# Zero products in TensorE's planned idle stretches, U transfers as single operations, and another score bank for the last tile

## The chip, the cores and the metric

The kernel runs on one core of one Trainium2 chip. The metric is the device time of one execution in microseconds (us). Before the change three runs took 506.69, 511.74 and 516.97 us; their median is 511.74 us. Profiles are of one execution each. Engines are named as in the profile: PE (TensorE's products), PEld (its weight loads), DVE (VectorE), ACT (ScalarE), POOL (GpSimd) and SP (SyncE, which here only issues transfers). A "q" behind an engine's name is its instruction sequencer.

## The reference, cut to what matters

```python
# A: attention with 16 query heads and one key and value head, S = 2048, D = 448, head size 28
q = (x @ wq).reshape(B, S, H, Dh).transpose(0, 2, 1, 3)
k = x @ wk
v = x @ wv
scores = jnp.einsum("bhqd,bkd->bhqk", q, k) * (Dh ** -0.5)
p = softmax(scores, axis=-1)
o = jnp.einsum("bhqk,bkd->bhqd", p, v)
a = o.transpose(0, 2, 1, 3).reshape(B, S, H * Dh) @ wo

# B: a state-space layer as a long convolution, L = 2048, D = 448 channels, N = 256 states
logdA = exp(log_dt)[:, None] * (A_re + 1j * A_im)
P = jnp.exp(logdA[:, :, None] * l[None, None, :])
K = jnp.einsum("dn,dnl,dn->dl", Cc, P, dB).real
y = causal_convolution(u, K) + u * Dskip          # by a Fourier transform in the reference

g = sigmoid((x * gate_w).sum(-1))
out = g * a + (1 - g) * b
```

## The kernel before, in words

**Attention.** The scores are cut into 1024 tiles of 128 keys by 512 query columns, grouped into 410 sets of three and two tiles in turn. `qk` (in `main`) makes a set: PE multiplies keys and queries into score banks of `psS` (L1264 for a set of three, as row-tiled products that run side by side; L1287 for single full products; L1275 and L1278 are the same two for the last 64 tiles, whose columns are cut in halves), and ACT takes the exponential of the whole set into the ring `expT` (L1313). There are five score banks, a tile's bank is its number modulo 5, so one set's products can be made while the other's exponential runs. `pv` (L1331, for the last 64 tiles L1325) multiplies four exponential tiles with the values and sums up in the one bank `psB` (bank 6) over the 16 key blocks of a head group. `norm` then copies that bank out (L1110), and further steps on DVE, POOL's transfers and PE divide by the row sums and project the output (`outp`, L1092). The last query block goes by `scaled` (L1154, L1161) and `last` (L1188, L1192, with the identity product that brings in what the output already holds), and its copy out of `psB` is L1341.

**State-space layer.** For each of 14 groups of 32 channels, `tables` builds tables of powers on DVE (L935, L950, L964 and others), `kgen` multiplies them on PE into the convolution's kernel (L994), and POOL stores this to a scratch tensor in memory, `KP_scratch`. `tload` brings it back as shifted copies: one table load is four transfer issues `T<-KP_scratch` on SP of 272 KB each, 56 loads in all (the late ones go into parts of `U` that are free by then, `U<-KP_scratch`). `conv` (L1054) is the convolution: products of `U`, the shifted inputs, with the loaded table, then DVE (L1063) and PE (L1074) turn the result for the output. `U` holds half of the channels. `ufill` refills a chunk of it for the second half from a copy in `T`: seven transfer issues `U<-T` on SP, a first one of 128 KB and six of 32 KB, in rows of 64 bytes. There are seven such chunks.

**Order.** Nothing is ordered by hand. Every step is recorded as an `Op` with an engine, a planned duration, a priority and its dependences, and `Prog.schedule` runs a list scheduler over all of them: it plays the program through with planned durations and puts each engine's instructions in the order in which they would start (`key = (r, o.pr, i)`). Each engine then executes its list strictly in that order, waiting on semaphores. A transfer counts as `ISSUE` (470 ns on SP) for each issue plus its landing time, and two transfers of one `slot` never overlap. The planner also keeps a model of PE's instruction fetch in blocks (`block`) and, for PE, of switches between tilings (`mode`, `SWITCH`).

PE has a filler already: behind the first 64 sets, `warm` (L1247) multiplies a matrix of 512 columns by columns of `cst` into `psB` with `start=False`, 43 times. Before the first work, L614 multiplies zeros of `cst` by themselves 18 times, L753 spreads one row over the partitions, and L624 turns the input.

Of the kernel before, what the change touches and what calls it, by code (L numbers as in the profile page):

```python
# [12 lines left out]
P = 128  # L13
# [63 lines left out]

class Op:
    __slots__ = ("i", "eng", "fn", "ns", "lat", "deps", "pr", "lock", "unlock", "slot", "ndma",
                 "count", "vc", "end", "comm", "extra", "mode", "ni")  # L80


class Prog:
# [9 lines left out]
    POOL = (7, 5)  # L93
    SLACK = {"pe": 500.0, "dve": 300.0}
    FAR = 2500.0

    def __init__(self, nc, es):
        self.nc, self.es = nc, es
        self.ops = []
        self.lastw = {}  # L100
        self.readers = {}
        self.slots = {}
        self.commops = {}
        self.after = {}

    def op(self, eng, fn, ns, rd=(), wr=(), pr=0, lat=None, lock=None, unlock=None, comm=None, mode="f", ni=0):
        o = Op()
        o.i, o.eng, o.fn, o.ns, o.lat, o.pr = len(self.ops), eng, fn, ns, 0, pr
        o.lock, o.unlock, o.slot, o.ndma = lock, unlock, None, 0
        o.comm = comm  # L110
        o.mode, o.ni = mode, ni
        o.lat = self.LAT[eng] if lat is None else lat
        deps = {}
        if comm is not None:
            for k in comm:
                deps[self.lastw[k]] = 1
                self.commops.setdefault(k, []).append(o.i)
        for k in rd:
            for c in self.commops.get(k, ()):
                deps[c] = 1  # L120
            w = self.lastw.get(k)
            if w is not None:
                deps[w] = 1
        for k in wr:
            w = self.lastw.get(k)
            if w is not None:
                deps[w] = 1
            for r in self.readers.get(k, ()):
                deps.setdefault(r, 0)
        for k in rd:  # L130
            self.readers.setdefault(k, []).append(o.i)
        for k in wr:
            self.lastw[k] = o.i
            self.readers[k] = []
        deps.pop(o.i, None)
        o.deps = deps
        self.ops.append(o)
        return o

    def dma(self, pairs, desc, slot, rd=(), wr=(), pr=0, eng="sp", slow=False, extra=0, fac=1.0):  # L140
        kw = dict(allow_slow_non_contiguous=True) if slow else {}

        def fn(e):
            return [e.dma_start(o, i, **kw) for o, i in pairs]  # L144
        nd, size = desc
        ns = 15.0 if size <= 64 else 13.0 + 0.033 * size if size < 1500 else 8.0 + 0.0372 * size
        o = self.op(eng, fn, nd * ns * fac / 16.0 * (1.15 if size < 1500 else 1.8 if nd < 512 else 1.0), rd, wr, pr)
        o.slot, o.ndma, o.extra = slot, len(pairs), extra
        prev = self.slots.get(slot)
        if prev is not None:  # L150
            o.deps[prev] = 1
        self.slots[slot] = o.i
        return o
# [11 lines left out]
    def schedule(self):  # L165
# [23 lines left out]
        done = 0  # L189
        npe = 0  # L190
        block = [0.0, 0.0]
        for o in ops:
            if o.eng == "pe":
                o.ni = self.count(o)
        while done < n:
# [24 lines left out]
            assert best is not None, "scheduler stuck"  # L220
            (r, _, _), e, i = best
            o = ops[i]
            ready[e].remove(i)
            if e == "pe" and o.mode != mode:
                r = max(r, free[e] + self.SWITCH)
                mode = o.mode
            if e == "pe":
                npe += o.ni
                while npe > self.FIRST + (len(block) - 2) * self.BLOCK:
                    block.append(r + (self.FETCH if dmafree > r else self.IDLE))  # L230
# [15 lines left out]
                o.lock.bank = L[3]  # L246
                L[2] = []
            if o.slot is not None:
                free[e] = r + self.ISSUE[e] * o.ndma
                s = r if e == "pool" else max(r, dmafree)  # L250
                end = max(s + o.ns, free[e]) + self.DMA_NS + o.extra
                dmafree = max(dmafree, s) + o.ns
            else:
                ns = o.ns
                if e == "pe" and self.HALF[0] < r < self.HALF[1]:
                    ns *= self.HALF[2]
                free[e] = r + ns
# [129 lines left out]
class Kernel:  # L387
# [182 lines left out]
    def prep_u(self):  # L570
# [15 lines left out]
        for k, (c0, c1) in enumerate(((0, 2), (2, 5), (5, 9), (9, 14))):  # L586
            n = 16 * (c1 - c0)
            pg.dma(self.ushift(self.U, 1024 * c0, self.U, 1024 * c0, 128, n, 1), (6 * 16 * n, 64), f"du{k}", rd=[("Ub", 0), ("Ub", 1)],
                   wr=[("Uc", c) for c in range(c0, c1)], pr=0.35 if k < 2 else 0.9 + 0.1 * k, slow=True)
        V0 = lambda b, off, n, r: b.v(0, P, off, [[n // r, r], [1, n // r]])  # L590
        Z = lambda n, r: self.cst.v(0, P, 512, [[0, r], [1, n // r]])
        pg.dma([(V0(self.O, 0, 16 * D, 32), Z(16 * D, 32))], (4096, 448), "zO", rd=[("cst", 1)] + done,
# [426 lines left out]
    def tload(self, gi):  # L1019
# [8 lines left out]
        for h in range(4):  # L1028
            to = bass.AP(tensor=buf.h, offset=h * rs + o, ap=[[4 * rs, 32], [TC, 8], [1, TC]])
            lst.append((to, dram(self.KP, h * 512 + 1 + 8 * gi * KW, [[1, 32], [KW, 8], [1, TC]])))  # L1030
        pg.dma(lst, (1024, 1088), f"T{s}", rd=[("KP", gi // 4, gi % 4 // 2), "pad", "kp0"] + x, wr=w, pr=1, extra=1500)

    def ufill(self, c):
        pg = self.pg
        lst = [(self.U.v(0, P, c * 2048, [[128, 16], [1, 32]]), self.T.v(0, P, UB + c * 512, [[32, 16], [1, 32]]))]
        lst += self.ushift(self.U, c * 2048, self.T, UB + c * 512, 32, 32, 1)
        pg.dma(lst, (5120, 64), f"uf{c % 4}", rd=[("UB", 0), ("UB", 1), ("yx", 2 * c + 5)], wr=[("Uc", 2 * c), ("Uc", 2 * c + 1)], pr=1.2, slow=True)

    def conv(self, c):
        pg = self.pg  # L1040
# [3 lines left out]
        for k in range(4):  # L1044
# [5 lines left out]
            for n in range(8):  # L1050
                def mm(e, k=k, n=n, to=to, gi=gi, tbuf=tbuf):
                    m0, par = 2 * (n // 2), n % 2
                    for j in range(4):
# [3 lines left out]
                                     start=(n == 0), stop=(n == 7), tile_position=(0, 32 * j), skip_group_check=True)  # L1057
                    return r
                first = k == 0 and n == 0
                pg.op("pe", mm, 56, mode="c", ni=8, rd=[("T", s), ("Uc", c % 14), ("Ub", 0), ("Ub", 1)],  # L1060
                      wr=[X] + ([("cst", cs)] if first else []), pr=1.6,
                      lock=ps if first else None)
        pg.op("dve", lambda e: e.tensor_tensor(self.cst.v(0, P, cs * 512, [[128, 4], [64, 2], [1, 64]]),  # L1063
# [107 lines left out]
    def last(self):  # L1171
        pg = self.pg
        for half in range(2):
            m1, m2 = self.scaled(half)
            for tt in range(2 * half, 2 * half + 2):
# [17 lines left out]
                                                                 tile_position=(0, 0), skip_group_check=True), 200,  # L1193
                          rd=[("O", tl), ("Oz", tl), "id"], wr=[Y] + key, pr=1, lock=F)
                if half:
                    pg.after[o.i] = end
                for g in range(3):
                    o = pg.op("pe", lambda e, mm=mm, g=g: mm(e, g), 200, rd=["Wo", ("on", g)],
                              wr=[Y] + key, pr=1)
# [26 lines left out]
    def main(self):  # L1226
# [13 lines left out]
        for ts in sets:  # L1240
            bs, es = sorted(t % 5 for t in ts), sorted(t % RING for t in ts)
            for t, b, x in zip(ts, bs, es):
                bank[t], ring[t] = b, x
        spread = lambda x, n: [[512 * (x[1] - x[0]), n], [1, 512]] if n > 1 else [[1, 512]]

        def warm(e):
            return e.matmul(self.psB.v(0, P, 0, [[1, 512]]), self.cst.v(0, P, 512, [[1, P]]),  # L1247
                            self.ident.v(0, P, 0, [[0, 4], [1, P]]), start=False, stop=False,
                            tile_position=(0, 0), skip_group_check=True)

        def qk(s):
            ts = sets[s]
# [64 lines left out]
        def pv(v):  # L1317
            ts = range(4 * v, 4 * v + 4)

            def mm(e):  # L1320
# [14 lines left out]
            pg.op("pe", mm, 230, rd=["va"] + [("e", ring[t]) for t in ts], wr=[("b", 6)], pr=0.5, mode="c", ni=8)  # L1335
            i, kt, h = dec(4 * v)
            if kt == 15 and i < 15:
                self.norm(i)
            if i == 15 and v % 8 == 7:
# [81 lines left out]
```

## Time and profile before

| | us |
|---|---|
| median of three runs | 511.74 |
| the profiled execution: time | 512.68 |
| its span, first to last instruction | 510.7 |
| PE busy / idle in the span | 443.5 / 67.2 |
| ACT busy | 485.6 |
| DVE busy | 457.6 |
| POOL busy | 167.5 |
| mean granted clock of PE, of full speed | 0.967 |

How to read it: busy time is the union of an engine's instructions. Ends of PE's products are modelled, so PE's busy time contains some of its pipeline. Rows of groups read "line engine operation, output<-input, shape xcount | busy us, mean ns of one | idle time of the engine just before them, and what ended it". Rows of the timeline begin with start and duration in us; a bracket at their end holds the engine's idle time before the row and what ended it. Neighbouring instructions of one line are merged in it ("x31"). `PEclk` is the clock that PE was granted, in tenths of full speed, over 40 equal slices of the span.

### The profile page before, as it was taken

The numbers are of one execution on the slowest core, as the hardware profiler recorded it, in microseconds if no ns is written. First come the engines' busy times: TensorE is split into PE (matmuls) and PEld (weight loads), VectorE is DVE, ScalarE is ACT, GpSimd is POOL, SyncE is SP. The second block draws the span as 40 slices with busy tenths as digits, with TensorE's granted clock in tenths as the row PEclk, the third lists the DMA queues.
The fourth block names the chain that finished last, engine by engine and source line by source line (L and its number), as shares of the span: only waits on it lengthen the run. The fifth ranks groups of instructions, "written<-read, shape, count | busy, mean of one in ns | idle before, by whom it ended". The sixth has DMA issues, their size and how long they took to land.

```text
span 510.7 us, 17103 instructions
## 1 busy us (share of the span) xinstructions
PE 443.5 (87%) x7468; PEld 202.9 (40%) x7558; DVE 457.6 (90%) x862; ACT 485.6 (95%) x435; POOL 167.5 (33%) x308
## 2 busy tenths in 40 slices
PE   8897788898888999889788979988888799899986
PEld 6522232243432445433343423443344243445552
DVE  5999999999999999999999969999999989992122
ACT  5999999999998999999999969999999899999984
POOL 5208334224133324215214223521514330624110
PEclk9799999999997999999999979999999799999999
DMA  8996399838427587974848666495672953777931
GB/s 259 323 167 176 40 201 147 246 91 256 135 60 250 144 235 143 300 149 111 176 142 251 135 215 151 110 321 119 187 167 86 300 132 133 217 230 211 338 98 45
DMA packets 151526, 91.84 MB, mean 180 GB/s; under 512 B 83514, under 2 KB 147436, under 8 KB 151452
## 3 DMA queue, kind: packets, MB, share of 16 engines
q1 hardware_dynamic: 141962, 81.05, 59.7%
q0 software_dynamic: 8960, 9.54, 7.8%
q8 instruction: 59, 0.97, 0.8%
q10 hardware_dynamic: 530, 0.17, 0.1%
q14 instruction: 15, 0.12, 0.1%
HBM read 73.61 MB, written 5.23 MB: 154 GB/s over the span
## 4 chain that ended last, share of the span: by engine, by line
ACT 57%; PE 22%; DVE 14%; DMA 4%; issue 2%; SPq 1%
ACT expT L1313 56%; DMA T<-KP_scratch 4%; PE psS L1287 4%; PE psS L1264 3%; DVE tab L935 3%; PE psB L1331 3%; PE psS L1054 2%; DVE tab L950 2%; PE psX L1054 1%; SPq L144 1%; PE psX L994 1%; PE psX L1092 1%; DVE tab L964 1%; PE psX L842 1%; DVE msq L881 1%
## 5 line engine op out<-in xcount | busy, mean ns | idle before, releaser
L1313 ACT ACTIVATE expT<-psS 128x1024 bf16<-128x1024 f32 (+1 forms) x410 | 466.7, 1336 | 13.4 <-PE psS L1264 6.8
L935 DVE TENSOR_TENSOR tab<-tab,mbf 128x512 bf16<-128x512 bf16 (+4 forms) x140 | 140.4, 1006 | 0.1
L1287 PE MATMUL psS<-qM,kT 128*128 128x512 bf16 x305 | 101.3, 393 | 24.9 <-ACT expT L1313 13.1
L1331 PE MATMUL psB<-expT,vaug 128*32 128x512 bf16 x960 | 97.4, 399 | 1.6 <-DVE acc L1110 1.3
L1264 PE MATMUL psS<-qT,kT 29*128 29x512 bf16 x570 | 76.7, 394 | 24.6 <-ACT expT L1313 22.8
L144 POOL DMA_DIRECT2D KP_scratch<-kstg x112 | 61.9, 559 | 104.9 <-DVE kstg L1004 104.6
L950 DVE TENSOR_TENSOR tab<-tab 128x256 bf16<-128x256 bf16 (+4 forms) x140 | 77.7, 578 | 0.0
L144 POOL DMA_DIRECT2D qM<-qT x64 | 32.3, 513 | 73.5 <-DVE qT L854 50.4
L1331 PEld LDWEIGHTS psB<-expT,vaug 128*32 128x32 bf16 x960 | 24.3, 93 | 78.4 <-issue 74.3
L144 POOL DMA_DIRECT2D rdenB<-R_scratch x60 | 31.2, 527 | 59.9 <-DMA R_scratch<-denT 59.8
L1264 PEld LDWEIGHTS psS<-qT,kT 29*128 29x128 bf16 x570 | 18.7, 91 | 67.6 <-ACT expT L1313 57.8
L1054 PE MATMUL psS<-T,U 128*26 128x128 bf16 (+3 forms) x1664 | 41.1, 229 | 4.2 <-DMA T<-KP_scratch 2.4
L1287 PEld LDWEIGHTS psS<-qM,kT 128*128 128x128 bf16 x390 | 24.1, 98 | 44.8 <-ACT expT L1313 29.9
L1054 PEld LDWEIGHTS psS<-T,U 128*26 128x26 bf16 (+3 forms) x1664 | 31.2, 109 | 20.3 <-issue 12.5
L1054 PE MATMUL psX<-T,U 128*26 128x128 bf16 (+3 forms) x1600 | 37.7, 225 | 1.1 <-DMA T<-KP_scratch 0.8
L1054 PEld LDWEIGHTS psX<-T,U 128*26 128x26 bf16 (+3 forms) x1600 | 28.5, 107 | 16.0 <-issue 9.5
L964 DVE TENSOR_TENSOR tab<-tab,tmp 128x1984 bf16<-128x1984 bf16 x28 | 32.3, 1186 | 0.1
L958 DVE TENSOR_TENSOR tmp<-tmp,mq 128x64 bf16<-128x64 bf16 (+4 forms) x70 | 25.9, 370 | 0.3
L881 DVE TENSOR_TENSOR msq<-seedz 128x512 f32<-128x512 f32 (+1 forms) x40 | 24.8, 621 | 0.0
L144 POOL DMA_DIRECT2D denT<-acc x15 | 11.5, 767 | 31.3 <-DVE acc L1110 29.2
L994 PE MATMUL psX<-tab 128*64 128x128 bf16 x480 | 21.0, 223 | 0.4 <-DVE kstg L1004 0.3
L144 POOL DMA_DIRECT2D R_scratch<-denT x15 | 8.9, 591 | 32.4 <-DVE denT L1116 16.0
(188 smaller groups left out, 492.3 us busy)
## 6 DMA issues: line engine op xcount, KB each, us to landing
T<-KP_scratch SPq DMA_DIRECT2D x204, 272.0 KB, 4.8
U<-KP_scratch SPq DMA_DIRECT2D x20, 272.0 KB, 5.4
rdenB<-R_scratch POOLq DMA_DIRECT2D x60, 64.0 KB
U<-cst SPq DMA_DIRECT2D x1, 3584.0 KB, 24.7
qM<-qT POOLq DMA_DIRECT2D x64, 32.0 KB, 4.1
tab<-in_A_x_dram SPq DMA_DIRECT2D x4, 448.0 KB, 5.1
O<-in_A_x_dram SPq DMA_DIRECT2D x16, 112.0 KB, 3.5
O<-cst SPq DMA_DIRECT2D x1, 1792.0 KB, 10.0
```

The source lines that it names most:

```text
L144: return [e.dma_start(o, i, **kw) for o, i in pairs]
L881: pg.op("dve", lambda e: e.tensor_tensor(m2(msq), z2, z2, ALU.mult), el(2 * n), rd=[kr, ki] + first, wr=["msq"], pr=pr)
L935: mul = lambda e, o, a, b: e.tensor_tensor(o, a, b, ALU.mult)
L950: vo(lambda e, dv=dv, tv=tv, k=k: e.tensor_tensor(dv, dv, tv, ALU.add if k else ALU.subtract), n, [kt[k], kd[k]], [kd[k]])
L958: vo(lambda e, w=w, lv=lv: e.tensor_tensor(rho.v(0, P, (32 - 2 * w) * 2, [[64, 32], [2, w], [1, 2]]), rho.v(0, P, (32 - w) * 2, [[64, 32], ...
L964: vo(lambda e, k=k: e.tensor_tensor(tab.v(0, P, FM + k * FP + 2, [[64, 32], [2, 31], [1, 2]]), tab.v(0, P, lm + k * PL + 62, [[64, 32], [- ...
L994: r = e.matmul(G.v(64 * u, 64, 128 * k, [[1, 128]]), tab.v(0, P, lo + comp * PL + cg * 64 + u, [[2, 64]]), tab.v(0, P, fo, [[64, 2], [mo - ...
L1054: r = e.matmul(ps.v(32 * j, 32 - m0, 128 * k, [[1, 128]]), self.U.v(0, P, (4 * gi + j) % UA // 2 * 128 + 2 * (2 * m0 + par) + j % 2, [[4, ...
L1264: r = e.matmul(self.psS.v(0, P, 512 * b, [[1, 512]]), kT.v(32 * h, DH + 1, 128 * kt, [[1, 128]]), qT.v(32 * h, DH + 1, 512 * (i % 2), [[1, ...
L1287: return e.matmul(self.psS.v(0, P, 512 * b, [[1, 512]]), kT.v(0, P, 128 * kt, [[1, 128]]), self.qM.v(0, P, (i % 2) * XQ + 512 * h, [[1, 51 ...
L1313: pg.op("act", lambda e: e.activation(expT.v(0, P, 512 * es[0], spread(es, n)), self.psS.v(0, P, 512 * bs[0], spread(bs, n)), AF.Exp, scal ...
L1331: r = e.matmul(self.psB.v(32 * h, 32, 0, [[1, 512]]), vaug.v(0, P, 32 * kt, [[1, 32]]), expT.v(0, P, 512 * ring[t], [[1, 512]]), start=(kt ...
```

## The change

Four things change.

1. **Zero products.** `main` hands the planner a `filler`: a product of 512 columns whose weights are a zero of `one`, summed into `psB` with `start=False`, so that it adds zeros. Whenever PE is to be given its next step, a sum in `psB` is open (`opened`: a product of `pv` has been placed and not the last one of its sum), PE would stand at least 215 ns plus the tiling switches less 50 ns (`w`), PE was busy less than 80% of the last 4 us of the plan, and no instruction fetch is due, the scheduler puts a filler there first.
2. **U transfers as single operations.** The seven issues of a `ufill` become seven operations that can be ordered apart, each planned at 1470 ns of SP's time. Their results are new keys `("Uf", chunk, j)`, which `conv` reads as well. The issues of `tload` are planned at 800 ns and those of the first fill of `U` (`du`) at 700 ns instead of 470.
3. **Last tile.** The last score tile, number 1023, uses bank 0 instead of bank 3.
4. **Last output tile.** Its identity product is put behind the last product of `pv` instead of behind the end of the first half.

As planned times change, the scheduler's order changes in many places on PE, POOL and SP.

```diff
-                 "count", "vc", "end", "comm", "extra", "mode", "ni")
+                 "count", "vc", "end", "comm", "extra", "mode", "ni", "psb", "iss")
...
+    FILL, FWIN, FLOW = 215.0, 4000.0, 0.8
...
+        self.filler = None
...
+        o.psb, o.iss = 0, self.ISSUE.get(eng)
...
-    def dma(self, pairs, desc, slot, rd=(), wr=(), pr=0, eng="sp", slow=False, extra=0, fac=1.0):
+    def dma(self, pairs, desc, slot, rd=(), wr=(), pr=0, eng="sp", slow=False, extra=0, fac=1.0, iss=None):
...
+        o.iss = o.iss if iss is None else iss
...
+            if e == "pe" and opened and self.filler is not None:
+                T = free[e]
+                j = (npe + 2 - self.FIRST - 1) // self.BLOCK + 1
+                w = self.FILL + (self.SWITCH if mode != "f" else 0.0) + (self.SWITCH if o.mode != "f" else 0.0) - 50.0
+                past = [x for x in past if x[1] > T - self.FWIN]
+                busy = sum(x[1] - max(x[0], T - self.FWIN) for x in past)
+                if r - T >= w and busy < self.FLOW * self.FWIN and (j >= len(block) or block[j] <= T):
+                    o = self.op("pe", self.filler, self.FILL, rd=["one", "id"], ni=2)
...
+                past.append((r, r + o.ns))
+                opened = o.psb == 1 if o.psb else opened
...
-                free[e] = r + self.ISSUE[e] * o.ndma
+                free[e] = r + o.iss * o.ndma
...
-                   wr=[("Uc", c) for c in range(c0, c1)], pr=0.35 if k < 2 else 0.9 + 0.1 * k, slow=True)
+                   wr=[("Uc", c) for c in range(c0, c1)], pr=0.35 if k < 2 else 0.9 + 0.1 * k, slow=True, iss=700.0)
...
-        pg.dma(lst, (1024, 1088), f"T{s}", rd=[("KP", gi // 4, gi % 4 // 2), "pad", "kp0"] + x, wr=w, pr=1, extra=1500)
+        pg.dma(lst, (1024, 1088), f"T{s}", rd=[("KP", gi // 4, gi % 4 // 2), "pad", "kp0"] + x, wr=w, pr=1, extra=1500, iss=800.0)
...
-        pg.dma(lst, (5120, 64), f"uf{c % 4}", rd=[("UB", 0), ("UB", 1), ("yx", 2 * c + 5)], wr=[("Uc", 2 * c), ("Uc", 2 * c + 1)], pr=1.2, slow=True)
+        for j, pair in enumerate(lst):
+            pg.dma([pair], (2048 if j == 0 else 512, 64), f"uf{j % 4}", rd=[("UB", 0), ("UB", 1), ("yx", 2 * c + 5)],
+                   wr=[("Uf", 2 * c, j), ("Uf", 2 * c + 1, j)], pr=1.2, slow=True, iss=1470.0)
...
-                pg.op("pe", mm, 56, mode="c", ni=8, rd=[("T", s), ("Uc", c % 14), ("Ub", 0), ("Ub", 1)],
+                pg.op("pe", mm, 56, mode="c", ni=8, rd=[("T", s), ("Uc", c % 14), ("Ub", 0), ("Ub", 1)] + [("Uf", c % 14, j) for j in range(7)],
...
-                    pg.after[o.i] = end
+                    pg.after[o.i] = end if tt == 2 else self.lastpv
...
+        bank[NTL - 1] = 0
...
+        def filler(e):
+            return e.matmul(self.psB.v(0, P, 0, [[1, 512]]), self.one.v(0, P, 2, [[0, P]]),
+                            self.ident.v(0, P, 0, [[0, 4], [1, P]]), start=False, stop=False,
+                            tile_position=(0, 0), skip_group_check=True)
+        pg.filler = filler
...
+            o = pg.op("pe", mm, 230, rd=["va"] + [("e", ring[t]) for t in ts], wr=[("b", 6)], pr=0.5, mode="c", ni=8)
+            self.lastpv = o.i
+            o.psb = 2 if kt == 15 or i == 15 and v % 8 == 7 else 1
```

More of the change, by code (lines that the diff above doesn't have):

```diff
@@ L191, in schedule @@
         block = [0.0, 0.0]
+        opened = False
+        past = []
         for o in ops:
@@ L222, in schedule @@
             o = ops[i]
+            if e == "pe" and opened and self.filler is not None:
[6 more added lines that the diff above has]
+                    o = self.op("pe", self.filler, self.FILL, rd=["one", "id"], ni=2)
+                    rt.append(0.0)
+                    need.append(0)
+                    succ.append([])
+                    n += 1
+                    i, r = o.i, T
+                    ready[e].append(i)
             ready[e].remove(i)
@@ L1334, in mm @@
                 return r
-            pg.op("pe", mm, 230, rd=["va"] + [("e", ring[t]) for t in ts], wr=[("b", 6)], pr=0.5, mode="c", ni=8)
             i, kt, h = dec(4 * v)
+            o = pg.op("pe", mm, 230, rd=["va"] + [("e", ring[t]) for t in ts], wr=[("b", 6)], pr=0.5, mode="c", ni=8)
+            self.lastpv = o.i
+            o.psb = 2 if kt == 15 or i == 15 and v % 8 == 7 else 1
             if kt == 15 and i < 15:
```

## The prediction

> **What bounds the kernel now.** I read the page first: parts 1 and 2, then the costliest group of part 5.
>
> ```profile
> PE 443.5 (87%) x7468; PEld 202.9 (40%) x7558; DVE 457.6 (90%) x862; ACT 485.6 (95%) x435; POOL 167.5 (33%) x308
> ...
> PEclk9799999999997999999999979999999799999999
> ...
> L1313 ACT ACTIVATE expT<-psS 128x1024 bf16<-128x1024 f32 (+1 forms) x410 | 466.7, 1336 | 13.4 <-PE psS L1264 6.8
> ```
>
> ACT is the bound: 410 exponentials of L1313 take 466.7 us one behind the other, and between them ACT stands only 13.4 us. No edit makes an exponential shorter, so 13.4 us is nearly all that there is to gain. The clock row has four dips (7, beside the 9s). The timeline of ACT says where the 13.4 us lie:
>
> ```profile
> 92.14 35.35 ACT L1313 ACTIVATE expT<-psS 128x1536 bf16<-128x1536 f32 x31 [0.81 <-PE psS L1264]
> 127.72 1.02 ACT L1313 ACTIVATE expT<-psS 128x1024 bf16<-128x1024 f32 x1 [0.24 <-PE psS L1287]
> 129.59 1.45 ACT L1313 ACTIVATE expT<-psS 128x1536 bf16<-128x1536 f32 x1 [0.84 <-PE psS L1264]
> 162.81 1.45 ACT L1313 ACTIVATE expT<-psS 128x1536 bf16<-128x1536 f32 x1 [1.25 <-PE psS L1264]
> 299.00 1.02 ACT L1313 ACTIVATE expT<-psS 128x1024 bf16<-128x1024 f32 x1 [2.63 <-PE psS L1287]
> 301.06 1.45 ACT L1313 ACTIVATE expT<-psS 128x1536 bf16<-128x1536 f32 x1 [1.04 <-PE psS L1264]
> 503.26 0.60 ACT L1313 ACTIVATE expT<-psS 128x512 bf16<-128x512 f32 x1 [0.48 <-PE psS L1278]
> ```
>
> The last bracket is ACT's idle time. Four more rows of this view belong to it: 0.48 and 0.37 at 302.99 and 304.39, and 0.70, 0.61 and 0.33 at 406.47, 408.10 and 410.84. I then asked for windows around them and halved these until the granted clock was one value in each:
>
> ```profile
> 47.40:50.80 3.40, 2.18 (x15) 0.45 (x15) 3.30 (x8) 3.40 (x4) 3.15 (x5) 1.00 0.14 24
> 84.95:88.36 3.41, 1.51 (x13) 0.41 (x12) 3.41 (x7) 3.41 (x4) 0.90 (x1) 1.00 0.82 226
> 153.21:156.62 3.41, 2.05 (x16) 0.52 (x16) 3.41 (x4) 3.41 (x5) 0.34 (x1) 1.00 1.00 319
> 88.36:91.77 3.41, 3.41 (x18) 0.71 (x15) 3.41 (x5) 2.96 (x3) 0.00 (x0) 0.50 1.11 278
> 156.62:163.45 6.83, 6.22 (x85) 2.45 (x88) 6.83 (x8) 5.53 (x6) 2.32 (x6) 0.50 0.80 266
> ```
>
> Columns are window, length, busy us of PE, PEld, DVE, ACT and POOL with counts, clock, DMA. The clock is 1.00 or 0.50, and it halves for one or two stretches of 3.41 us right behind a stretch in which PE was busy little: 1.51 us (share 0.44) before 88.36, 1.95 (0.57) before 125.90, 2.05 (0.60) before 156.62, 1.16 before 296.56, 2.24 (0.65) before 402.41. Stretches of 2.18 (0.64) at 47.40 and 2.15 (0.63) at 54.23 passed. While the clock is halved a product takes 0.61 us in the timeline instead of 0.39 and ACT waits for PE; all other waits of ACT but a few of 0.1 to 0.5 us and one of 1.19 at 490.25 are in the last stretch. The dip at 296.56 has another root, in SP's and PE's timelines:
>
> ```profile
> 278.77 10.29 SPq L144 DMA_DIRECT2D U<-T  x7
> 279.44 4.75 SPq L144 DMA_DIRECT2D U<-T  x1
> 297.26 0.30 PE L1054 MATMUL psS<-T,U 128*32 128x128 bf16 x4 [2.39 <-DMA T<-KP_scratch]
> ```
>
> Seven U transfers held SP for 10.29 us, 4.75 of them the second issue alone; the table load (four issues of `T<-KP_scratch`) stood behind them from 289.11, its last part landed at 297.22, and PE, which runs its list in order, stood 2.39 us with the score products queued behind the convolution.
>
> **The change part by part.** Terms are for ACT, the path that sets the end.
>
> *Zero products.* The changed order has 137 of them, singly and in runs of up to four, and places 4 to 5 in each of the stretches before 88.36, 125.90, 156.62 and 402.41 (counted between the same exponentials). The nearest row is the existing filler L1247 (x43, 389 ns modelled); behind it the next product starts 0.22 us later (92.02 to 92.24), so I take 0.22 us each. Four add 0.88 us: 0.44 becomes 0.70, 0.60 becomes 0.86, 0.65 becomes 0.90, all above the 0.63 that passed. That zeros count as work is shown at the start of the trace: L614 multiplies zeros by zeros from 1.14 to 5.16 at 420 ns for 256 columns, and a product of 448 columns at 6.66 takes 0.36 us, as 448 columns do at clock 1.00 (L1092, 357 ns). So the four dips go: 0.81 + (0.24 + 0.84) + 1.25 + (0.70 + 0.61 + 0.33) = 4.78 us off.
>
> The Trainium skill, "TensorE: Matmul & The Clock Gate", section "HAM oscillation — how this bites in real kernels", words its rule as no idle gaps of PE above about 3.4 us. Here the longest gap in the stretches before 88.36 and 125.90 is 0.74 us, and the clock halved all the same, so the trace goes by the share of the stretch, not by the gap. By the page's rule short gaps would not matter, and nothing of the 4.78 us would be the fillers' to save.
>
> Cost of the fillers: 137 x 0.22 = 30.1 us of PE, to be hidden in the 67.2 us that PE stands (510.7 - 443.5). The cover is PE's wait for ACT to free a score bank: 57.8 and 29.9 us in the page's list of waits before the weight loads of L1264 and L1287. A filler that starts late delays the next score product by up to 0.22 us; this one ends 0.6 us after its bank comes free (0.61 for two at L1287), while ACT has 1.02 or 1.45 us of the other exponential to do, so 0.4 us of slack takes it. I put 0 to 5 us on it (one in six on the path) and take 0.23, one more wait of the small kind (65.85 and 79.00 have 0.23 each).
>
> *U transfers.* Seven issues of one chunk may now stand apart, each costed at 1470 ns in the order's making, T issues at 800. Queue work stays: 49 U issues, 224 loads from KP. What moves is order on SP: the load that stood behind the fourth chunk now stands some 16 us ahead of its use in the planner's own times, so the stall at 297.26 and its dip should go: 2.63 + 1.04 + 0.48 + 0.37 = 4.52 us off. Against that, loads now stand directly behind a chunk's first piece (128 KB) in the second and third chunk, or behind one or two pieces. The queue's rows say what an issue behind the first piece costs: 4.5 to 5.5 us in six chunks, 1.01 in one (311.11), where SP had been quiet. The load of the second chunk is due 0.4 us after its planned landing. At 1.01 it waits for nothing; at 4.75 it is 4.1 us later than at 0.63, less 0.84 by which the piece and 0.17 x 4 = 0.68 by which the load are costed above their rows: 2.6 us behind its plan, 2.2 beyond the 0.4, a stall as the old one of 2.39. The new reading of `Uf` adds waits of PE on transfers that end 80 us before use: nothing. Bounds: 0 to 4.52; I take 0.41, ACT's wait at 217.70 behind four crowded loads, since the load before now starts some 4 us earlier and the queue is then half drained. On POOL a few stores swap places with other small transfers; these feed steps tens of us later: nothing.
>
> *Last tile.* Its product (L1278 at 502.83) waits for the two-tile exponential before it, whose banks are 3 and 4. In bank 0 it waits for the three-tile one, which is issued earlier, so the last exponential follows without its 0.48 us. The late identity product of the last output tile fits while PE waits for the copy of L1341 (0.51 us of idle before L1154): nothing, at worst 0.2.
>
> Sum on the profiled execution: 510.7 - 4.78 - 4.52 - 0.48 + 0.23 + 0.41 = 501.6 us span. That execution took 512.68, 1.98 beyond its span, so **503.5 us**. It lies 0.94 above the median of 511.74. Where the stretches fall against the work differs between executions, so the number of dips should too; this fits runs from 506.69 to 516.97, and a kernel without dips should scatter less.
>
> **The rivals.** 2% of 511.74 is 10.2 us, about what tells a change from none: below 501.5 is faster, above 522.0 slower.
>
> *More than the rows show* (chance 0.30). Of 13.4 us, 3.6 are not in the sum (13.4 - 9.78): 0.41 at 217.70, 0.54 at 444.47, 1.19 at 490.25 and small ones. Dips shift everything behind them, so part of these may go. For: the fastest run of before, 506.69, still has the stall at 297.26, which sits in the order; 506.69 - 4.52 - 0.48 = 501.7, and any dip of that run comes off too. Against: the wait at 490.25 is PE standing 1.6 us for nothing that the profile names, while the outputs are stored. Time: 503.5 - 3.6 to 503.5 - 2.1, 499.9 to 501.4.
>
> *The stall only moves* (0.17). The load behind the first U piece of the second chunk is 2.2 us late, PE stands, the clock halves again: the 4.52 come back in place of the 0.41, 503.5 + 4.1 = 507.6 us. For: six of seven rows. Against: the spacing.
>
> *Dips stay* (0.06). The rule by gaps of the page named above, or zeros that count for nothing: 503.5 + 4.8 = 508.3 us. Against: dips behind gaps of 0.74 us, and L614.
>
> *Slower: the fillers sit on PE's path* (0.07). They are placed by planned idle, and the real idle is smaller: PE's gaps in the timeline are 0.20 and 0.74 us where the plan has 0.36 and 0.90. Where PE runs late, each filler pushes the score products by 0.22 us, 0.44 at half clock. If all did, 503.5 + 30 = 533 us. It ends slower when 18.5 us reach ACT, that is 84 of 137. For: PE is 87% busy. Against: those durations contain the modelled ends, and 0.4 us of slack comes back with each exponential.
>
> **How the numbers follow.** The forecast, 501.5 to 506.5, gets what is left: 0.40. Range: from 499.5, the low end of the first rival, to 509.5, which takes in the moved stall, the remaining dips and 1.2 us of both; outside lie the slower case and little else. Faster by over 2%: 0.30 from the first rival and 0.04 from the forecast's own edge, 0.34; slower 0.07; within 2% 0.59.
>
> **What would show it.** Right: no 7 in the clock row from slice 6 to 36, L1313's idle down from 13.4 to some 4 us, no wait of PE for `T<-KP_scratch` near 297, no idle before the last exponential. Wrong: a PE wait for `T<-KP_scratch` behind a first U piece (near 227); dips behind well filled stretches; many waits of 0.2 us before L1313 with a filler ahead of the score product.

## The result and the profile after

| | before | after |
|---|---|---|
| median, us (executions) | 513.37 (20) | 505.13 (20) |
| lowest to highest, us | 506.01 to 516.97 | 503.15 to 508.18 |
| ratio of compared runs, 95% interval | | 0.9916 (0.989 to 0.9943) |
| the profiled execution: time, span | 512.68, 510.7 | 508.04, 506.0 |
| mean granted clock in it | 0.967 | 0.987 |

The time fell by 0.84% in the compared runs, less than the 2% that counts as faster. The medians alone give 505.13 / 513.37 = 0.984; the ratio is nearer to 1 because the comparison leaves out executions over 1.5% above the fastest of their kernel, and of the kernel before that is ten of the 20 (among the 68 below, whose clocks are on record, those left out had the clock halved for 37.7 us on average, the others for 25.2). Two repeats gave 0.9897 (0.9857 to 0.9937) and 0.9916 (0.9883 to 0.9948). The 37 executions of the changed kernel have a median of 505.17; the 68 of the kernel before in three batches have 511.1, from 505.43 to 520.05.

The page of the changed kernel: busy times, the clock row, and the rows of the exponential and of the new filler (busy us, mean ns of one, idle before).

```profile
PE 467.7 (92%) x7600; PEld 214.2 (42%) x7695; DVE 456.1 (90%) x862; ACT 486.0 (96%) x435; POOL 166.2 (33%) x308
...
PEclk9799999999999999999999999999999999999979
...
L1344 ACT ACTIVATE expT<-psS 128x1024 bf16<-128x1024 f32 (+1 forms) x410 | 467.1, 1315 | 8.4 <-PE psS L1306 2.4
...
L1277 PE MATMUL psB<-ident,one 128*128 128x512 bf16 x137 | 44.0, 383 | 0.0
```

Between slices 6 and 36 the clock row has no 7 any more; there is a new one at 39. The exponentials are as long as before (467.1 us, 466.7 before), and their idle time fell from 13.4 to 8.4 us: the span's 4.7 us are this row. Windows of the same execution, the first four over the filled stretches (length, busy us of PE, PEld, DVE, ACT and POOL with counts, clock, DMA):

```profile
85.00:88.40 3.40, 2.63 (x20) 0.90 (x20) 3.40 (x8) 3.40 (x4) 0.90 (x1) 1.00 0.90 213
122.50:125.90 3.40, 3.19 (x49) 1.37 (x47) 3.40 (x10) 3.40 (x4) 0.60 (x2) 1.00 0.99 298
152.00:155.40 3.40, 3.31 (x22) 0.83 (x19) 3.40 (x5) 3.40 (x4) 2.00 (x4) 1.00 1.02 363
390.00:393.40 3.40, 3.32 (x26) 0.85 (x23) 3.40 (x3) 3.40 (x4) 1.53 (x4) 1.00 1.05 360
479.60:483.00 3.40, 1.34 (x38) 0.85 (x32) 0.42 (x1) 1.95 (x2) 1.98 (x4) 1.00 0.22 61
483.00:489.80 6.80, 6.80 (x126) 4.50 (x124) 1.06 (x3) 4.09 (x4) 0.00 (x0) 0.50 0.08 25
```

The first four hold 2.63 us of PE or more, where before 1.5 to 2.2 us stood, and the clock stays at 1.00 in them. The last dip lies behind a stretch with 1.34 us. Its cause is in the timelines of PE and SP (start, duration; the bracket is the idle time before):

```profile
479.66 0.39 PE L1306 MATMUL psS<-qT,kT 29*128 29x256 bf16 x6
482.11 0.48 PE L1078 MATMUL psS<-T,U 128*32 128x128 bf16 x20 [2.06 <-issue]
...
```

```profile
471.83 32.08 SPq L147 DMA_DIRECT2D out_dram<-O  x7
```

PE stood 2.06 us for nothing that the profile names. Before, the same wait was 1.59 us at 489.25; both times output stores were running. In ACT's timeline the gain and this loss stand beside each other:

```profile
116.22 89.76 ACT L1344 ACTIVATE expT<-psS 128x1536 bf16<-128x1536 f32 x79 [0.19 <-PE psS L1295]
206.15 103.47 ACT L1344 ACTIVATE expT<-psS 128x1024 bf16<-128x1024 f32 x91 [0.17 <-PE psS L1318]
...
483.17 1.02 ACT L1344 ACTIVATE expT<-psS 128x1024 bf16<-128x1024 f32 x1 [1.62 <-PE psS L1309]
485.44 1.45 ACT L1344 ACTIVATE expT<-psS 128x1536 bf16<-128x1536 f32 x1 [1.25 <-PE psS L1306]
487.25 1.02 ACT L1344 ACTIVATE expT<-psS 128x1024 bf16<-128x1024 f32 x1 [0.36 <-PE psS L1309]
489.20 9.88 ACT L1344 ACTIVATE expT<-psS 128x1536 bf16<-128x1536 f32 x9 [0.93 <-PE psS L1306]
```

From 116.22 to 309.62 two rows hold 170 exponentials, with 0.17 us of idle time between them; before, the dips at 125.9 and 156.6 and the stall at 297 lay in that stretch. The last row runs to the last exponential, so the 0.48 us ahead of that one is gone. The wait of PE costs ACT 1.62 + 1.25 + 0.36 + 0.93 = 4.16 us.

### The profile page after: what moved, and what is told of

It reads as the page before. It is cut to its first block, busy times and chain, and to the rows that moved or that the text cites. A ratio compares the mean times of both kernels' runs of the same rounds, so it can differ in the third digit from the quotient of the medians.

```text
span 506.0 us, 17377 instructions
## 1 busy us (share of the span) xinstructions
PE 467.7 (92%) x7600; PEld 214.2 (42%) x7695; DVE 456.1 (90%) x862; ACT 486.0 (96%) x435; POOL 166.2 (33%) x308
## 4 chain that ended last, share of the span: by engine, by line
DVE 51%; ACT 32%; PE 12%; issue 2%; DMA 1%; SPq 0%
ACT expT L1344 31%; DVE tab L957 14%; DVE tab L972 7%; DVE msq L903 3%; DVE tab L986 3%; DVE tmp L980 2%; DVE mbf L923 2%; DVE kstg L1026 2%; DVE seedz L907 2%; DVE seedz L905 2%; PE psS L1078 2%; PE psS L1295 1%; DMA T<-KP_scratch 1%; DVE qT L876 1%; DVE cst L1087 1%
## 5 line engine op out<-in xcount | busy, mean ns | idle before, releaser
L1344 ACT ACTIVATE expT<-psS 128x1024 bf16<-128x1024 f32 (+1 forms) x410 | 467.1, 1315 | 8.4 <-PE psS L1306 2.4
L1318 PE MATMUL psS<-qM,kT 128*128 128x512 bf16 x300 | 97.2, 382 | 14.4 <-issue 11.4
L1362 PE MATMUL psB<-expT,vaug 128*32 128x512 bf16 x960 | 95.2, 389 | 1.1 <-DVE acc L1134 0.7
L1295 PE MATMUL psS<-qT,kT 29*128 29x512 bf16 x570 | 75.5, 387 | 7.5 <-ACT expT L1344 4.0
L1277 PE MATMUL psB<-ident,one 128*128 128x512 bf16 x137 | 44.0, 383 | 0.0
L1078 PE MATMUL psS<-T,U 128*26 128x128 bf16 (+3 forms) x1664 | 39.8, 224 | 3.1 <-issue 2.4
L1078 PEld LDWEIGHTS psS<-T,U 128*26 128x26 bf16 (+3 forms) x1664 | 30.1, 107 | 19.8 <-issue 13.8
L1078 PE MATMUL psX<-T,U 128*26 128x128 bf16 (+3 forms) x1600 | 36.5, 221 | 1.5 <-issue 0.8
L1016 PE MATMUL psX<-tab 128*64 128x128 bf16 x544 | 23.7, 223 | 1.3 <-issue 0.7
```

Source lines behind the costliest of these rows:

```text
L1078: r = e.matmul(ps.v(32 * j, 32 - m0, 128 * k, [[1, 128]]), self.U.v(0, P, (4 * gi + j) % UA // 2 * 128 + 2 * (2 * m0 + par) + j % 2, [[4, ...
L1277: return e.matmul(self.psB.v(0, P, 0, [[1, 512]]), self.one.v(0, P, 2, [[0, P]]), self.ident.v(0, P, 0, [[0, 4], [1, P]]), start=False, st ...
L1295: r = e.matmul(self.psS.v(0, P, 512 * b, [[1, 512]]), kT.v(32 * h, DH + 1, 128 * kt, [[1, 128]]), qT.v(32 * h, DH + 1, 512 * (i % 2), [[1, ...
L1318: return e.matmul(self.psS.v(0, P, 512 * b, [[1, 512]]), kT.v(0, P, 128 * kt, [[1, 128]]), self.qM.v(0, P, (i % 2) * XQ + 512 * h, [[1, 51 ...
L1344: pg.op("act", lambda e: e.activation(expT.v(0, P, 512 * es[0], spread(es, n)), self.psS.v(0, P, 512 * bs[0], spread(bs, n)), AF.Exp, scal ...
L1362: r = e.matmul(self.psB.v(32 * h, 32, 0, [[1, 512]]), vaug.v(0, P, 32 * kt, [[1, 32]]), expT.v(0, P, 512 * ring[t], [[1, 512]]), start=(kt ...
```

## The experiments

Two quantities are used throughout. *Halved time* of an execution is 2 x (1 - mean granted clock) x span, the time at a clock of 0.50. A straight line through the 68 executions of the kernel before gives time = 502.5 + 0.303 us for each us of halved time (95% 0.249 to 0.358). Nearly all have the start's first stretch near 20 us, some 6.8 us long (6 of the 37 executions of the changed kernel have 1 us or less in all); the mean is 27.4 for the kernel before and 6.4 for the changed one. The line's lowest execution stands at 10.1 us, so at 6.4 it is carried a little beyond its data.

### Each part by itself

The first kernel has the fillers (135 of them), and everything else as before:

```diff
-        for j, pair in enumerate(lst):
-            pg.dma([pair], (2048 if j == 0 else 512, 64), f"uf{j % 4}", ...
-                   wr=[("Uf", 2 * c, j), ("Uf", 2 * c + 1, j)], pr=1.2, slow=True, iss=1470.0)
+        pg.dma(lst, (5120, 64), f"uf{c % 4}", ...
...
-                    pg.after[o.i] = end if tt == 2 else self.lastpv
+                    pg.after[o.i] = end
...
-        bank[NTL - 1] = 0
```

> The kernel before plus the zero products alone (108 or more of them; U transfers, planned issue costs, last tile and last output tile as before). Theory A, the parts add up as forecast (dips 4.8 us, stall behind the U transfers 4.5 us, last tile 0.5 us): median about 4.8 us under before, some 508.5 us; no halved clock except at the start and around one wait of PE for T<-KP_scratch behind a U chunk, which stays with 2 to 2.7 us of ACT idle behind it. Theory B, the zero products do all of it and the stall only showed because a dip stood behind it: about 8 us under before, as after (505). Theory C, the U order does all of it: within 1.5 us of before, dips still there.

507.67 us (502.72 to 513.28, 12 executions), ratio 0.9925 (0.9883 to 0.9966); halved time 7.5 us on average. So the fillers alone end the dips, but 2.5 us above the whole change. PE's timeline of its profiled execution (510.42 us, a long one) shows waits that can account for it:

```profile
215.05 0.59 PE L1076 MATMUL psX<-T,U 128*32 128x128 bf16 x28 [1.47 <-DMA T<-KP_scratch]
...
382.94 0.30 PE L1076 MATMUL psX<-T,U 128*32 128x128 bf16 x4 [1.82 <-DMA T<-KP_scratch]
```

There is no stall near 297: the fillers changed the planned times, and with them SP's order. Two waits for table loads stand elsewhere, and the second has a dip behind it (ACT stood 1.65 + 0.95 us from 384 on). A third of 0.83 us is at 329.23, and at 485.03 PE stood 1.71 us for nothing that the profile names, which cost ACT 2.02 + 0.71 us.

The second kernel is the changed one without its fillers (`pg.filler = filler` taken out): transfer order, costs and last tile alone.

> The changed kernel without its zero products. Theory A: the wait for T<-KP_scratch near 297 us is gone, dips of the clock stay, some four or five per execution; 4.5 to 5 us under before, some 508.5 us, and a spread as wide as before's. Theory B: within 1.5 us of before. Theory C: as after, 505 us.

513.11 us (509.43 to 519.37, 12 executions), ratio 1.0056 (1.0017 to 1.0094): slower than before, which no theory had. The page of its fastest execution:

```profile
PEclk9799799999997999999998799999999799999999
```

Four dips follow the start's, in slices 5, 13, 23 and 32. There is no stall near 297: in ACT's timeline 40 exponentials run without a wait from 285.75 to 331.47. But this kernel's halved time is 39.4 us on average, 12 more than before, and by the line's price that is 12 x 0.303 = 3.6 us. Without it the kernel would stand at 509.5, some 1.6 us better than before. So the transfers' order is worth something, and without fillers the new order of PE's list gives it back in dips. Why this order has more of them stays open.

The third takes only the splitting of the U transfers back; the fillers (137) and the planned costs stay:

```diff
-        for j, pair in enumerate(lst):
-            pg.dma([pair], (2048 if j == 0 else 512, 64), f"uf{j % 4}", ...
+        pg.dma(lst, (5120, 64), f"uf{c % 4}", rd=[("UB", 0), ("UB", 1), ("yx", 2 * c + 5)], ..., iss=1470.0)
```

> The changed kernel with a U chunk again as one operation of seven issues, still planned at 1470 ns each; zero products and all else as after. Theory K (what counts is the planned cost, which puts the loads in time): within 1 us of after. Rival L (the splitting counts): waits of PE for T<-KP_scratch of 1 us and more come back, 2 us and more slower than after, as in the run with zero products alone (507.7).

508.24 us (505.06 to 512.9, 12 executions), ratio 0.997 (0.9932 to 1.0008); halved time 8.8 us. The time is that of the theory that splitting matters, the mechanism isn't: there is no wait of a us for a table load. PE's timeline has two waits of the other kind instead:

```profile
471.42 0.26 PE L1304 MATMUL psS<-qT,kT 29*128 29x256 bf16 x1 [1.46 <-issue]
...
484.30 0.38 PE L1076 MATMUL psX<-T,U 128*30 128x128 bf16 x13 [2.39 <-issue]
```

ACT lost 1.50 and 2.05 us there. What one part brings depends on where the scheduler's list then puts everything else.

### Is the stall in the order, and what is left of it

Both kernels unchanged, on another chip. First the kernel before:

> The kernel before once more, for a second profile. Theory A (the stall near 297 us comes from the order on SP and is in every execution): PE waits again 1.5 us or more for T<-KP_scratch behind the fourth U chunk, and ACT 2 us or more behind it. Rival H (it was a chance of the one profiled execution): PE's wait there is under 0.8 us. In both cases three to six dips of the clock, at other places than in the first profile.

508.13 us. PE's timeline of that execution:

```profile
294.55 0.25 PE L1054 MATMUL psS<-T,U 128*32 128x128 bf16 x4 [2.55 <-DMA T<-KP_scratch]
```

The stall of 2.39 us at 297.26 is here 2.55 us at 294.55, and the wait ahead of the last exponential 0.48 at 498.69. Three dips stand behind the start, at 154.9, 294.8 and 366.5. The second follows the stall again, and the first lies close to the one at 156.62; those at 88.36, 125.90 and 402.41 are missing, and 366.5 is new. So the stall and the last wait are in the order, and the dips differ between executions, though not all of them.

Then the changed kernel:

> The changed kernel once more, beside the other runs of this call. 505 us, 503 to 508; no halved clock after 40 us, or one dip near 483 us behind PE's wait for instructions. If the price of a dip is as the runs of before have it (0.30 us for each us of halved clock, by a line through 23 runs), it runs where that line stands at the 7 us of the start: 504.8 us.

505.12 us (503.62 to 505.84, 6 executions); the profiled one has a span of 503.0, no dip behind the start, and 5.0 us of idle time before L1344. Its SP and PE show the rival "the stall only moves" in small:

```profile
216.92 0.62 SPq L147 DMA_DIRECT2D U<-T  x1
217.74 6.63 SPq L147 DMA_DIRECT2D T<-KP_scratch  x4
224.41 6.57 SPq L147 DMA_DIRECT2D U<-T  x6
```

```profile
229.59 0.25 PE L1078 MATMUL psS<-T,U 128*32 128x128 bf16 x4 [0.60 <-DMA T<-KP_scratch]
```

Behind the first U piece of the second chunk the four issues of a load take 6.63 us, where the planned costs give 3.2; the load lands late, PE stands 0.60 us and ACT 0.28. Of the seven profiles of this order with single fillers, four have this wait, at 0.28 to 1.01 us of ACT, and three have none, the first among them. The four issues took 5.4 to 7.0 us in all seven, 6.60 in the first, so their length alone does not decide whether PE waits.

A third set of executions of the changed kernel went with the last batch:

> The changed kernel beside the three others of this call: 505.1 us, 503 to 508; PE's wait before the convolution near 482 us between 0.4 and 2.1 us (0.95 and 2.06 in the two profiles so far).

505.42 us (503.4 to 506.84, 11 executions). Its PE stood at the same place as in the first profile, 2.06 us at 483.30, and ACT lost 1.62 + 0.26 us, since no dip followed.

### Does the wait at 480 come from the output stores

The three large output stores on SP get one more input, a result of the final part, so that they start later. Nothing else changes. First behind the last norm of half the tiles:

```diff
-   rd=[("O", 4 * qc + k) for k in range(4)], pr=1)
+   rd=[("O", 4 * qc + k) for k in range(4)] + [("nx", 0)], pr=1)
```

> The changed kernel with the first three output stores waiting for the second product of the first half of the last query block (some 488 us) instead of starting at 472 us. Theory F, PE's unexplained wait of 2.06 us at 480 us is its instruction fetch held up by these stores on the DMA engines: the wait falls under 0.5 us, the dip at 483 us goes, the profiled execution loses some 4 us of ACT idle time, and the median falls by 1 to 2 us to some 503.5 us. Rival G, the wait has another cause: it stays, and the median stays at 505 or rises by up to 2 us as the stores end later.

504.67 us (502.59 to 507.27, 6 executions), ratio 0.99 (0.9852 to 0.9947). The stores are issued from 484.74; PE's wait at 480 is gone and one of 0.41 at 475.72 is left. Then behind the last convolution, `("yx", 27)` in place of `("nx", 0)`:

> The same with the three stores waiting for the last turning product of the last convolution (some 493 us). Theory F: no PE wait at 480, 1 to 2 us under after, unless the stores now end last; the stores need some 8 us each from issue to landing, overlapped, so they should land before 506 us. Rival G: as after or up to 3 us slower, the end set by out_dram.

504.28 us (502.03 to 505.86, 6 executions), ratio 0.9884 (0.9837 to 0.9931), and the same kernel again beside the third set of the changed one:

> The kernel with the three output stores behind the last convolution again, to be compared with the changed kernel in this same call: 504.2 us, 0.5 to 1.2 us under it if PE's wait for instructions near 482 us is all that the gating removes; no difference if that wait is rare.

503.5 us (503.28 to 505.38, 6 executions), ratio 0.9877 (0.982 to 0.9934), against 0.9916 for the changed kernel in that batch. The timelines of PE, SP and ACT in the second set:

```profile
479.88 0.39 PE L1306 MATMUL psS<-qT,kT 29*128 29x256 bf16 x6
480.20 0.48 PE L1078 MATMUL psS<-T,U 128*32 128x128 bf16 x20
```

```profile
488.99 10.46 SPq L147 DMA_DIRECT2D out_dram<-O  x7
```

```profile
468.94 25.69 ACT L1344 ACTIVATE expT<-psS 128x1536 bf16<-128x1536 f32 x23
```

The same two products follow each other without a gap, the stores run from 488.99 on, and ACT goes through its last 23 exponentials without a wait. The 12 executions have a median of 503.73, 1.44 us below the 37 of the changed kernel (95% -2.1 to -0.3, by resampling both). This version beats both kernels. That holding the stores back removes the wait is shown. Stores are not the only thing that brings such waits: the kernel with unsplit U transfers has one at 471.42 with its stores issued from 475.16 only, and the one with few fillers has one of 1.91 us at 330.10 with no store near.

What PE waits for can be read from the record of DMA packets, which the changed kernel's page sums up by queue (packets, MB, share):

```profile
q8 instruction: 60, 0.98, 0.8%
```

These are packets of 16 KB, one for every 255 of the 7600 + 7695 instructions of PE and PEld; the kernel before has 59 for 7468 + 7558, also 255 each. So this queue carries PE's program. Each of the waits ends 1.3 to 1.6 us after one of its packets has landed:

| profile | packet landed, us | PE went on, us | PE had stood, us |
|---|---|---|---|
| changed kernel, first | 480.64 | 482.11 | 2.06 |
| changed kernel, second | 480.20 | 481.80 | 0.95 |
| changed kernel, third | 481.87 | 483.30 | 2.06 |
| kernel before, first | 487.78 | 489.25 | 1.59 |
| unsplit U transfers | 470.11 | 471.42 | 1.46 |
| unsplit U transfers | 483.02 | 484.30 | 2.39 |
| few fillers | 328.50 | 330.10 | 1.91 |

The packet near 480 is the 57th. In the three profiles of the changed kernel it starts 5.7 to 6.9 us behind the 56th; in the three profiles with the stores held back it starts 3.5 to 4.4 us behind it, and PE does not wait. So PE stands because its next instructions are not there yet, and they come later while the stores run. How the stores delay the packet stays open.

### What the fillers cost, and what they do

The filler product made twice (274 in place of 137), the order unchanged:

```diff
+            for _ in range(2):
+                r = e.matmul(self.psB.v(0, P, 0, [[1, 512]]), ...
+            return r
```

> The changed kernel with each zero product made twice (274 products, 30 us more of PE), the planned time of 215 ns and so the whole order unchanged. Theory S (0.4 us of slack behind each exponential takes a late filler): within 1.5 us of after, 505 to 506.5 us. Rival P (the fillers sit on PE's path): each doubled filler in a planned gap of 165 to 215 ns delays the score products by 0.2 us; if a third reach ACT, some 10 us slower, 515 us.

516.87 us (515.25 to 518.4, 6 executions), ratio 1.0129 (1.0091 to 1.0168): 11.75 us more than the changed kernel for 137 x 0.22 = 30 us more of PE. The clock is not the cause (halved time 5.1 us). A place in PE's timeline and what follows in ACT's:

```profile
257.33 1.04 PE L1278 MATMUL psB<-ident,one 128*128 128x512 bf16 x4
258.30 0.39 PE L1297 MATMUL psS<-qT,kT 29*128 29x512 bf16 x3
```

```profile
258.73 3.77 ACT L1346 ACTIVATE expT<-psS 128x1536 bf16<-128x1536 f32 x3 [0.46 <-PE psS L1297]
```

Where two fillers stood now stand four, the score product behind them starts late, and ACT waits 0.46 us; the idle time before the exponentials is 12.8 us, 5.0 with single fillers, and they themselves took 470.2 us in place of 466.8.

Now the filler with 256 columns in place of 512:

```diff
-            return e.matmul(self.psB.v(0, P, 0, [[1, 512]]), self.one.v(0, P, 2, [[0, P]]),
-                            self.ident.v(0, P, 0, [[0, 4], [1, P]]), start=False, stop=False,
+            return e.matmul(self.psB.v(0, P, 0, [[1, 256]]), self.one.v(0, P, 2, [[0, P]]),
+                            self.ident.v(0, P, 0, [[0, 2], [1, P]]), start=False, stop=False,
```

> The changed kernel with zero products of 256 columns instead of 512; planned time and order unchanged, so PE has 15 us less of them. Theory S2 (single fillers lie in PE's waits and cost ACT next to nothing; only doubled ones outgrow their gaps): no gain from shorter ones, 504.5 to 505.5 us if they still hold the clock, and 1 to 3 us more where dips come back (halved clock above 10 us per execution). Rival P2 (fillers cost ACT in proportion to their length, 11.7 us for 30 us more in the doubled run): 15 us less give up to 5.9 us back, 499 to 501 us.

505.13 us (503.34 to 506.91, 12 executions): no gain from 15 us less of PE. Its halved time is 8.8 us, 2.4 more than with full fillers, worth 0.7 us by the line; so the full fillers may cost some 0.7 us more than the half ones, with about 1 us of uncertainty either way between the two medians.

Last, fewer of them: the planner fills only where PE was busy less than 60% of the last 4 us (`FLOW` 0.6 in place of 0.8), which leaves 36.

> The changed kernel with FLOW at 0.6 instead of 0.8: 36 zero products instead of 137, only where the plan has PE busy less than 60% of 4 us. Theory: what closes the gate is a stretch of 3.4 us filled to less than some 0.45 in the plan; none of these is left with 36 fillers either, so dips stay rare: halved clock under 12 us per execution, 504.5 to 506.5 us. Rival: the threshold lies higher, near 0.6, so half of the dips come back: 15 to 20 us halved, 507 to 509 us.

506.92 us (505.27 to 511.71, 12 executions), ratio 0.9961 (0.9919 to 1.0003), halved time 14.2 us: between the two theories. A window ahead of one of its dips, and the same place in PE's timeline:

```profile
389.90:393.30 3.40, 2.12 (x17) 0.61 (x17) 3.40 (x6) 3.40 (x5) 2.50 (x5) 1.00 0.49 128
393.30:396.70 3.40, 3.40 (x13) 0.78 (x13) 3.40 (x2) 2.85 (x4) 0.00 (x0) 0.50 0.98 340
```

```profile
391.16 0.61 PE L1318 MATMUL psS<-qM,kT 128*128 128x512 bf16 x2 [0.20 <-ACT expT L1344]
392.51 0.39 PE L1295 MATMUL psS<-qT,kT 29*128 29x512 bf16 x3 [0.74 <-ACT expT L1344]
```

A stretch with a share of 2.12 / 3.40 = 0.62 and no gap above 0.74 us halves the clock. With 137 fillers that place holds four of them, 3.32 us of PE, and the clock stays.

## Where the prediction was right, and which step failed

The measured 505.13 lies in the range of 499.5 to 509.5, and the forecast of a gain below 2% held. The gain was put too high: 503.5 / 511.74 = 0.984, a gain of 1.6%, against the measured 0.9916, a gain of 0.84%. That the two medians of the result differ by 513.37 - 505.13 = 8.24 us, exactly the forecast 511.74 - 503.5, is luck: the 68 later executions of the kernel before have a median of 511.1, so the difference is 5.9 us.

The step that failed is the term for the U transfers, 4.52 us off with 0.41 against it, together with the last tile's 0.48. It took the old stall off and put what the new order costs ACT at other places at next to nothing. The runs showed the stall gone and no net gain from these parts. The paragraphs below give the numbers.

**Dips: right, and the whole of the gain.** The four filled stretches keep the clock, and so does nearly every execution: 6.4 us of halved time in place of 27.4. At 0.303 that is (27.4 - 6.4) x 0.303 = 6.4 us, as much as the medians' 511.1 - 505.2 = 5.9. The rival by the rule on gaps falls: dips come behind stretches of gaps up to 0.74 us, and products of zeros hold the clock. The Trainium skill, "TensorE: Matmul & The Clock Gate", section "HAM oscillation — how this bites in real kernels", also puts the cost of halved time at half of it. Here it is 0.30. A likely reason, which no run tested, is that ACT sets the end and score banks that are already full cover part.

**The sum's base: an execution with more dips than most.** "Sum on the profiled execution" took every dip of one execution as the change's to save. That execution had 34 us of halved time, 6.6 more than the mean of 68 executions, worth 2.0 us. In the forecast time this cancels, since the dips taken off are those of the same execution: 4.78 us and, within the U transfers' term, 1.04 + 0.48 + 0.37 = 1.89 us, together 6.67. That this comes so near the 6.4 us of the mean execution is partly luck: 6.67 us for the 26.9 us of halved time behind the start is 0.25 for each, where the line has 0.303. The text saw that the dips differ between executions, and did not ask for their mean, which the clock of more runs would have given.

**U transfers and last tile: the step that failed.** Without its dip, the U transfers' term leaves 2.63 us for the stall; with the last tile's 0.48, and 0.23 and 0.41 against them, the forecast has 2.47 us apart from the dips. In no profile of the changed order is there a stall near 297. But at the changed kernel's halved time the line of the kernel before gives 504.5 us (95% 503.4 to 505.7), and the changed kernel has 505.2: of the 2.47 us nothing is left, half a us at most. The profiles show where it went. The sum leaves 13.4 - 9.78 + 0.23 + 0.41 = 4.3 us of idle time before the exponentials; the three profiles of the changed kernel have 8.4, 5.0 and 6.9. In place of the stall ACT waits 0 to 0.9 us near 230 (0.41 in the sum), 0.2 to 0.4 near 330 and 0 to 0.6 near 404, and the wait at 480 grew. These named waits make some 1.5 to 2 us; the rest stays open.

**The wait at 490.25: left standing, and it grew.** The first rival named it as one that speaks against more gain, and the sum kept it at 1.19 us. In three profiles of the changed kernel it cost ACT 4.16 (with the dip that it caused), 0.62 and 1.88. What PE waits for there, its own instructions, was not in the prediction. Holding the stores back takes the wait out, and the two profiled spans of that kernel are 500.6 and 501.6 us, the second just the sum's. That they agree is partly luck, as the sum's other errors show.

**Last tile: right for this order only.** The 0.48 us is gone in the three profiles of the changed kernel. But it is there in the kernel without fillers (0.48 at 500.15) and in the one with few (0.49 at 496.57), both with bank 0, and is absent with the fillers alone and bank 3. The shapes in the timelines say when: the wait comes where the exponential right before the last one holds its bank, a two-tile one with bank 3, a three-tile one with bank 0. Which of them comes last is the scheduler's choice.

**Fillers on PE's path: nearly free, as far as was tested.** Halving them changes nothing that can be measured, and 0.23 us was put on them. What their presence costs is less sure: with its dips priced, the kernel without fillers stood 1.6 us better than the kernel before, and the one with them does not. Part of the missing gain may be the fillers' own; no run separates it from the list's other order. The argument of 0.4 us of slack for each filler was too generous as a general rule: with a second one at each place 11.75 of 30 us reached ACT, where 0.4 us of slack would have covered a further 0.22. The planned gaps fit one filler each, and hardly more.

## What to carry to other kernels

A term that comes from the clock is to be sized from the mean granted clock of many executions, not from the dips of one profile. Zero products hold the clock where PE's share of a stretch of 3.4 us is low, and halving their length gave no time back, so single ones that fit a planned gap cost little; doubled, they cost 11.75 us. In a kernel ordered by a list scheduler the parts of a change do not add up, since each one moves the whole list: they are to be priced together, and waits at the old places and at new ones read from the trace again. Where the profile names no reason for a wait of PE, it helps to ask when the last packet of the instruction queue landed.

## What the runs showed of the hardware

- The clock halves by PE's share in a stretch of about 3.4 us: in the windows shown it fell behind shares of 0.39 (1.34 of 3.40 us) and 0.62, and stayed with 0.77 (2.63 of 3.40) and more. Between these the share alone does not decide: in the kernel before it stayed behind 0.63 and 0.64 and fell behind 0.65. In the changed kernel the windows were laid where the dips had been, since no change of clock marks the stretches there. Products whose weights are zeros count as work, and those of 256 columns nearly as well as those of 512 (halved time 8.8 and 6.4 us).
- PE can stand 0.4 to 2.4 us with no wait that the timeline names. In the seven cases of 0.95 us and more in the table above it went on 1.3 to 1.6 us after a 16 KB packet of the instruction queue had landed. Near the end of the kernel this packet came later while output stores ran, and holding these back took the wait away, for 1.44 us of the whole.
- Four issues of a table load behind a 128 KB U piece in rows of 64 bytes took 6.63 us on SP (5.4 to 7.0 in seven profiles), and four with no such piece ahead took 2.55 us (the kernel before in its second profile, at 273.94).
